# Pooled attention with a hierarchical mixture of experts: the router's weights, the guess of the first expert, one copy chain, one subtraction and one down piece change places in a hand-written order

## The chip, the cores and the metric

The kernel runs on one core of one Trainium2 chip. The metric is the device time of one execution in microseconds (us). Engines are named as in the profile: PE (matmuls; PEld is its weight load), DVE, ACT, POOL, and SP, which issues most of the transfers.

## The reference

Eight batches of attention whose k and v are averaged over groups of 8 positions (576 positions become 72), and behind them a mixture of 4 groups of 4 experts that sends each of the 4608 tokens to one expert.

```python
k_p = k.reshape(B, H, Sp, pool, D).mean(axis=3)          # 8, 8, 72, 64
v_p = v.reshape(B, H, Sp, pool, D).mean(axis=3)
scores = scale * np.matmul(q, k_p.transpose(0, 1, 3, 2))
scores = scores - np.max(scores, axis=-1, keepdims=True)
attn = np.exp(scores)
attn = attn / (np.sum(attn, axis=-1, keepdims=True) + 1e-09)
x = np.matmul(attn, v_p)                                 # then (4608, 512)
...
g_idx = np.argmax(x @ w_group, axis=1)                   # group of each token
...
e_idx = np.argmax(xg @ w_expert[g], axis=1)              # expert within the group
...
h = np.maximum(xg[mask_e] @ w1[g, e], 0.0)               # 512 -> 1024
out[tok_idx] = combined[:, None] * (h @ w2[g, e])        # 1024 -> 512
```

## The kernel before

**Tiling.** A batch has 576 tokens in five chunks (four of 128, one of 64), two chunks side by side in the scores' tiles. One expert, guessed from the mean of v, is computed for all tokens of a batch; the tokens that chose another expert are done at the end. Each fp32 operand of the up (512 to 1024) and down (1024 to 512) matmuls is cut into a high and a low part, and a product is made of three matmuls.

**The order is written by hand.** Four strings name small pieces of work, and `run` calls them one by one; the scheduler keeps that order on each engine, so a piece's instructions stand on each engine's list where the string has it. START opens batch 0's attention and fetches the first expert's weights; FIRST is the rest of batch 0 with its experts, together with batch 1's attention; STEADY serves batches 1 to 6 and LAST batch 7. In them `a` and `m` are the attention and the experts of the batch at hand, `n` and `w` those of the next one, `x` the attention after that, `t` the router's weights and the idle matmuls.

**The pieces that matter here**, with the profile's lines:

- `load_wr` fetches the router's weights by two transfers that ACT issues (L894 the groups', 8 KB, L895 the experts', 32 KB; tile `ht`). `turn_wr` transposes them on PE (L901), `put_wr` copies them (L904, ACT).
- `qt`, `qta`: q of one chunk transposed (L298, PE) and copied (L304, ACT). `sc`: scores (L320, PE). `mx`, `sb`: maximum and its subtraction (L326, L333, DVE). `ex`: exponential (L337, ACT). `su_`: sums and reciprocals (L342 to L344, DVE). `nm`: division (L349, POOL). `pt`: transpose (L355, DVE).
- `vr`: sums of v over 8 positions (L223 is the last addition on POOL). `rep`: these sums repeated over the partitions by matmuls (L244, L247, PE); `repa` and `repd` copy them (L253, ACT; L261, DVE).
- `guess_x` (L483 on PE, a copy L485 on ACT) and `guess_e` (L491 on PE; then DVE from L494 to L472 and L475): the expert of most tokens, guessed. SP reads its number, and `load` (L549) fetches its weights in pieces of 512 KB.
- `av`: probabilities by v (L375, PE), here in two runs for each batch: `av:0:1` and `av:2:4` in batch 0, `av:0:4` in two parts in batch 1. `ava` takes the high part (L389, ACT), `avd` the low one (L393, DVE).
- `split`: high part of an expert's weights (L556, ACT); `spd`: their low part (L562 on DVE, L566 on POOL). `up` (L579, PE), `ua` (L584, ACT), `upd` (L589, DVE).
- `down:z`: 8 matmuls (L618; L623 for the last chunk); z counts in threes through the chunks, so 0 to 2 are chunk 0, 9 to 11 chunk 3; 12 and 13 are the last chunk. `da` takes a finished chunk from PSUM (for the last chunk ACT L634, DVE L635, ACT L636).
- `warm:z`: z matmuls whose result nobody reads (L911).

Tiles of one name go round in a pool (`mm` and `sc` in PSUM): a piece that opens one waits until the one before it in that place has been read.

Of the kernel before, what the change touches and what calls it, by code (L numbers as in the profile page):

```python
# [34 lines left out]
TCARGS = dict(schedule_with_timeline_sim=True)  # L35

START = """
a.load_k:1:w a.load_k:0:w a.load_q:0 a.qt:0 a.load_r:k a.load_r:v a.load_q:1 a.kr:0:r a.kr:1:p a.load_v:0 a.load_v:1 a.rr:r a.qta:0 a.load_q:3 a.kt
n.load_r:v t.load_wr a.kta a.qt:1 a.load_q:4 a.vr:0:r a.sc:0 a.mx:0 t.turn_wr a.qta:1 a.vr:1:p a.sc:1 a.load_q:2 t.warm:2 a.sb:0 n.load_r:k a.ex:0
n.load_k:0 a.mx:1 t.put_wr a.sb:1 a.su_:0 a.qt:3 a.ex:1 a.rep a.guess_x a.nm:0:p a.su_:1 a.repd:1 a.repa:1 a.nm:1:p n.load_v:1 a.pt:0 a.repa:0 a.qt:2  # L40
a.repd:0 a.qta:3 n.load_k:1 a.pt:1 a.guess_e n.kr:0:r a.av:0:1 a.ava:0:0 a.ava:0:1 a.avd:0:1 a.ava:0:3 a.qt:4 m.load:1:1 m.load:1:2 m.load:1:3
a.ava:0:2 a.qta:2 a.sc:3 a.avd:0:3 a.avd:0:0 m.load:1:0 a.avd:0:2 n.kr:1:p a.mx:3 a.sb:3 m.split:1:1 a.ex:3 n.load_qb:3 m.spd:1:1:v n.load_qb:1 a.sc:2
a.su_:3 t.warm:4 a.nm:3:p a.qta:4 t.warm:7
"""
FIRST = """
m.split:1:3 a.mx:2 m.up:2:0 n.load_qb:2 m.split:1:2 m.ua:2:0 a.sc:4 a.sb:2 t.warm:8 m.spd:1:2:p m.up:3:0 a.pt:3 m.up:4:0 m.up:5:0 a.ex:2 a.mx:4 a.sb:4
# [5 lines left out]
m.split:2:2 x.load_k:0 x.load_qb:0 m.up:3:1 x.load_k:1 m.ua:6:1 m.ua:3:1 n.ex:1 x.load_v:1 m.split:2:0 n.su_:0 a.count m.up:1:1 n.repa:1 m.up:2:1  # L52
m.upd:6:1 n.sc:3 n.repd:1 m.split:2:1 n.sc:4 m.ua:2:1 n.su_:1 m.up:0:1 a.keep_x m.ua:1:1 n.repd:0 n.nm:0:p m.upd:3:1 n.nm:1:p m.upd:2:1 m.spd:2:1:p
m.up:5:1 m.up:4:1 n.mx:4 n.pt:0 m.upd:1:1 n.mx:3 m.spd:2:0:p n.pt:1 m.down:0 n.sb:3 n.sb:4 m.ua:5:1 n.ex:3 m.ua:0:1 n.ex:4 m.ua:4:1 m.upd:5:1
m.upd:0:1 n.su_:4 m.spd:2:2:p n.nm:4:p m.upd:4:1 a.gex n.su_:3 n.nm:3:p m.down:12 x.kr:1:p n.pt:4 m.down:13 n.pt:3 n.av:0:4:0 n.av:0:4:1 x.load_qb:2
x.load_qb:1 n.ava:0:1 x.kr:0:r x.load_v:0 m.down:1 x.rr:r a.gates n.ava:0:4 n.ava:0:0 n.ava:0:3 n.ava:0:2 n.avd:0:4 n.avd:0:0 x.vr:1:p n.avd:0:3
m.da:4 n.avd:0:2 m.down:2 n.xr:0 m.down:9 n.xr:3 x.kt x.qb:0 n.ava:0:5 n.avd:0:1 n.avd:0:5 x.kta n.xr:2 m.down:6 x.vr:0:r x.sc:0 n.xr:1 n.rt x.rep
x.mx:0 x.sb:0 n.route x.repa:0 x.repd:1 m.down:10 n.main_expert w.load:1:0 x.ex:0 m.da:0 n.gex w.load:1:1 x.su_:0 m.down:11 x.repa:1 w.load:1:3
m.down:3 m.down:4 w.load:1:2 x.qb:1 x.repd:0 m.down:7 n.gates w.load:2:1 w.split:1:0 m.da:3 w.load:2:0 x.nm:0:p m.down:5 w.spd:1:0:v n.keep_x x.pt:0
# [902 lines left out]
```

## Time and profile before

| what | value |
|---|---|
| three executions | 550.5, 552.46, 553.12 us; median 552.46 |
| the profiled execution | 555.95 us, of which span from first to last instruction 554.3 |
| mean granted clock of PE | 0.994 of full speed |
| PE busy | 532.4 us, 96% of the span |
| DVE, POOL, ACT busy | 359.2 (65%), 275.7 (50%), 214.9 us (39%) |
| chain that ended last | PE 89%, DVE 5%, DMA 2%, ACT 1%, issue 1% |

The chain that ended last is followed back from the last instruction to what released it, step by step, and its shares say which engine the time was spent on. PE is idle for some 22 us, and its slices of busy time in the profile's second part are under 9 tenths only at the opening and at the end.

### The profile page before, as it was taken

What the parts mean: (1) busy time and instruction counts of PE and PEld (TensorE: products, weight loads), DVE (VectorE), ACT (ScalarE), POOL (GpSimd) and SP (SyncE); (2) the same over time, 40 slices, a digit from 0 to 9 for tenths busy, and PEclk for the clock granted to TensorE, in tenths of its full rate; (3) what the DMA queues carried; (4) which work ended last, traced back from release to release, by engine and by line L of the source; (5) the groups of instructions that cost most, each with busy time, mean ns of one, the idle gap of its engine ahead of it and who ended that gap; (6) DMA issues with size and microseconds to landing.
All of it is one profiled execution on the core that took longest, in us unless ns stands there. A gap on an engine that the chain in (4) does not pass through costs nothing.

```text
span 554.3 us, 15239 instructions
## 1 busy us (share of the span) xinstructions
PE 532.4 (96%) x6218; PEld 472.7 (85%) x6218; DVE 359.2 (65%) x940; ACT 214.9 (39%) x402; POOL 275.7 (50%) x259
## 2 busy tenths in 40 slices
PE   4889998999999999999999999999999999999995
PEld 3789987799888998899888998899888997899874
DVE  4688897678385946858485946857485944347520
ACT  2254523245324543345334533354324532344111
POOL 3527386116942668046933678146933654165400
PEclk9999998999999999999999999999999999999998
DMA  9778561299108751389109740499309000634801
GB/s 235 157 187 199 144 124 51 92 304 203 40 21 290 209 97 56 124 275 192 41 20 332 181 103 35 151 392 201 58 20 355 19 1 21 235 136 182 293 22 72
DMA packets 115649, 81.32 MB, mean 147 GB/s; under 512 B 73562, under 2 KB 92250, under 8 KB 115192
## 3 DMA queue, kind: packets, MB, share of 16 engines
q1 hardware_dynamic: 110256, 70.92, 46.0%
q10 hardware_dynamic: 5288, 9.35, 4.5%
q8 instruction: 50, 0.82, 0.6%
q14 instruction: 23, 0.19, 0.1%
q0 software_dynamic: 32, 0.04, 0.0%
HBM read 75.01 MB, written 28.38 MB: 187 GB/s over the span
## 4 chain that ended last, share of the span: by engine, by line
PE 89%; DVE 5%; DMA 2%; ACT 1%; issue 1%; POOL 0%; SPq 0%; POOLq 0%
PE mm L579 35%; PE mm L618 31%; PE sc L375 5%; PE mm L623 5%; PE sc L320 4%; PE tp L409 1%; DMA rem<-in_k_dram 1%; DMA ht<-in_moe_w_expert_dram 1%; PE mm L598 1%; PE sc L244 1%; PE mm L911 1%; DVE su L342 1%; DVE p L333 1%; DVE mx L326 1%; DVE pT L355 1%
## 5 line engine op out<-in xcount | busy, mean ns | idle before, releaser
L579 PE MATMUL mm<-xt,w 128*128 128x256 f32 (+1 forms) x1536 | 214.9, 298 | 0.1
L579 PEld LDWEIGHTS mm<-xt,w 128*128 128x128 f32 x1536 | 206.5, 189 | 5.4 <-DVE ht L589 1.8
L618 PE MATMUL mm<-w,ht 128*128 128x512 f32 x744 | 177.9, 394 | 0.0
L566 POOL TENSOR_TENSOR w<-sw,w 128x512 fp32r<-128x512 f32 x94 | 120.5, 1307 | 92.9 <-ACT w L556 62.7
L618 PEld LDWEIGHTS mm<-w,ht 128*128 128x128 f32 x744 | 137.5, 188 | 31.1 <-issue 2.8
L349 POOL TENSOR_TENSOR p<-p,su 128x576 f32<-128x576 f32 (+1 forms) x40 | 45.8, 1152 | 124.6 <-DVE su L344 117.4
L589 DVE SCALAR_TENSOR_TENSOR ht<-mm,ht 128x256 fp32r<-128x256 f32 x192 | 57.5, 342 | 65.6 <-ACT ht L584 65.4
L584 ACT ACTIVATE ht<-mm 128x320 fp32r<-128x320 f32 (+1 forms) x128 | 51.3, 412 | 109.8 <-PE mm L579 109.3
L556 ACT CAST w<-sw 128x1024 fp32r<-128x1024 f32 x64 | 66.1, 1045 | 20.0 <-DMA sw<-in_moe_w_dram 19.9
L326 DVE TENSOR_REDUCE mx<-sc 128x8 f32<-128x576 f32 (+1 forms) x40 | 29.8, 745 | 34.3 <-PE sc L320 34.3
L400 POOL TENSOR_TENSOR sw<-xt 128x640 f32<-128x640 f32 (+1 forms) x28 | 39.1, 1426 | 10.5 <-DVE xt L393 10.4
L218 POOL TENSOR_TENSOR kv<-kv 128x512 f32<-128x512 f32 x21 | 32.0, 1524 | 9.6 <-DMA kv<-in_v_dram 7.5
L337 ACT ACTIVATE p<-p 128x576 f32<-128x576 f32 (+1 forms) x40 | 27.3, 682 | 23.1 <-DVE p L333 21.7
L375 PE MATMUL sc<-pT,v 32*64 32x128 f32 (+11 forms) x1560 | 33.3, 297 | 2.7 <-issue 2.0
L355 DVE STREAM_TRANSPOSE pT<-p 128x576 f32<-128x576 f32 (+1 forms) x40 | 30.6, 764 | 7.3 <-POOL p L349 7.2
L631 ACT ACTIVATE y<-mm,gm 128x512 f32<-128x512 f32 x31 | 21.3, 689 | 31.8 <-PE mm L618 23.1
L375 PEld LDWEIGHTS sc<-pT,v 32*64 32x64 f32 (+3 forms) x1560 | 28.5, 143 | 6.0 <-issue 3.8
L623 PE MATMUL mm<-w,ht 128*128 128x512 f32 x128 | 31.7, 391 | 0.0
L342 DVE TENSOR_REDUCE su<-p 128x8 f32<-128x576 f32 (+1 forms) x40 | 29.4, 735 | 3.2 <-ACT p L337 3.2
L333 DVE TENSOR_TENSOR p<-sc,mx 128x576 f32<-128x576 f32 (+1 forms) x40 | 29.9, 748 | 1.0
L320 PE MATMUL sc<-kT,qT 64*64 64x72 f32 x1264 | 28.3, 237 | 1.5 <-DVE xt L393 1.4
L389 ACT CAST xt<-sc 128x480 fp32r<-128x480 f32 (+3 forms) x36 | 18.0, 542 | 29.7 <-PE sc L375 15.5
(217 smaller groups left out, 490.9 us busy)
## 6 DMA issues: line engine op xcount, KB each, us to landing
sw<-in_moe_w_dram SPq DMA_DIRECT2D x72, 512.0 KB
xscr<-xt SPq DMA_DIRECT2D x8, 2304.0 KB
kv<-in_v_dram SPq DMA_DIRECT2D x16, 512.0 KB
q<-in_q_dram SPq DMA_DIRECT2D x112, 72.0 KB
out_dram<-y ACTq DMA_DIRECT2D x31, 256.0 KB
kv<-in_k_dram SPq DMA_DIRECT2D x14, 512.0 KB
kv<-in_moe_w_dram SPq DMA_DIRECT2D x6, 512.0 KB
pT<-xscr SPq DMA_DIRECT2D x2, 1152.0 KB
```

The lines of the kernel that those rows point to most:

```text
L320: nc.tensor.matmul(ps[t:t + 64, y, SP * g:SP * g + SP], lhsT=s.qT[c][r, g, w:w + 64], rhs=k, start=True, stop=True)
L349: (nc.vector if eng == "v" else nc.gpsimd).tensor_tensor(out=pf, in0=pf, in1=bc(sf, SP), op=ALU.mult)
L355: nc.vector.transpose(out=s.pT[0:n, :, 32 * c:32 * c + 32], in_=s.p[c].rearrange("p u x s -> p (u x s)").rearrange("p (b i) -> p b i", i=3 ...
L375: nc.tensor.matmul(to[64 * x:64 * x + 64], lhsT=w, rhs=s.pT[e, k, 32 * c0:32 * c0 + n], start=(z == 0), stop=(z == 2))
L400: nc.gpsimd.tensor_tensor(out=x, in0=a, in1=b, op=ALU.add)
L556: nc.scalar.copy(out=wh, in_=raw)
L566: nc.gpsimd.tensor_tensor(out=wl[:, p], in0=raw[:, p], in1=wh[:, p].bitcast(F32), op=ALU.subtract)
L579: nc.tensor.matmul(ps[:, 0:n], lhsT=l[:, kc, fs], rhs=xt[:, r, kc, sl], start=(kc == 0 and i == 0), stop=(kc == 3 and i == 2))
L584: nc.scalar.activation(out=s.ht[f][:, o:o + n], in_=s.pu[f, hf][:, 0:n], func=AF.Relu)
L589: stt(out=ht[:, at:at + hi - lo], in0=ps[:, lo - o:hi - o], scalar=0.0, in1=ht[:, lo:hi].bitcast(F32), op0=ALU.max, op1=ALU.subtract)
L618: nc.tensor.matmul(ps, lhsT=s.ht[f][:, 640 * l + o:640 * l + o + 128], rhs=s.w[2, f // 2][r][:, f % 2, :], start=(i == 0), stop=(i == 23))
L623: nc.tensor.matmul(ps, lhsT=s.ht[f][:, 512:640], rhs=s.w[2, f // 2][r][:, f % 2, :], start=(i == 0), stop=(i == 15))
```

## The change

START is rewritten and two lines of FIRST are; no piece is added, and only `t.warm:7` becomes `t.warm:3`. In the diff, moved pieces have shifted the line breaks:

```diff
 START = """
-a.load_k:1:w a.load_k:0:w a.load_q:0 a.qt:0 a.load_r:k a.load_r:v a.load_q:1 a.kr:0:r a.kr:1:p a.load_v:0 a.load_v:1 a.rr:r a.qta:0 a.load_q:3 a.kt
-n.load_r:v t.load_wr a.kta a.qt:1 a.load_q:4 a.vr:0:r a.sc:0 a.mx:0 t.turn_wr a.qta:1 a.vr:1:p a.sc:1 a.load_q:2 t.warm:2 a.sb:0 n.load_r:k a.ex:0
-n.load_k:0 a.mx:1 t.put_wr a.sb:1 a.su_:0 a.qt:3 a.ex:1 a.rep a.guess_x a.nm:0:p a.su_:1 a.repd:1 a.repa:1 a.nm:1:p n.load_v:1 a.pt:0 a.repa:0 a.qt:2
-a.repd:0 a.qta:3 n.load_k:1 a.pt:1 a.guess_e n.kr:0:r a.av:0:1 a.ava:0:0 a.ava:0:1 a.avd:0:1 a.ava:0:3 a.qt:4 m.load:1:1 m.load:1:2 m.load:1:3
-a.ava:0:2 a.qta:2 a.sc:3 a.avd:0:3 a.avd:0:0 m.load:1:0 a.avd:0:2 n.kr:1:p a.mx:3 a.sb:3 m.split:1:1 a.ex:3 n.load_qb:3 m.spd:1:1:v n.load_qb:1 a.sc:2
-a.su_:3 t.warm:4 a.nm:3:p a.qta:4 t.warm:7
+t.load_wr a.load_k:1:w a.load_k:0:w a.load_q:0 a.qt:0 a.load_r:k a.load_r:v a.load_q:1 a.kr:0:r a.kr:1:p a.load_v:0 a.load_v:1 a.rr:r a.qta:0
+a.load_q:3 a.kt n.load_r:v a.kta a.qt:1 a.load_q:4 a.vr:0:r a.sc:0 a.mx:0 t.turn_wr a.qta:1 a.vr:1:p a.sc:1 a.load_q:2 t.warm:2 a.sb:0 n.load_r:k
+a.ex:0 n.load_k:0 a.mx:1 t.put_wr a.sb:1 a.su_:0 a.ex:1 a.guess_x a.qt:3 a.rep a.nm:0:p a.su_:1 a.repd:1 a.repa:1 a.nm:1:p n.load_v:1 a.pt:0 a.repa:0
+n.load_k:1 a.guess_e a.qt:2 a.repd:0 a.qta:3 a.pt:1 n.kr:0:r a.av:0:1 a.ava:0:0 a.ava:0:1 a.avd:0:0 a.ava:0:2 a.qt:4 m.load:1:1 m.load:1:2 m.load:1:3
+a.ava:0:3 a.qta:2 a.sc:3 a.avd:0:1 a.avd:0:2 m.load:1:0 a.avd:0:3 n.kr:1:p a.mx:3 m.split:1:1 m.spd:1:1:v a.sb:3 a.ex:3 n.load_qb:3 n.load_qb:1 a.sc:2
+a.su_:3 t.warm:4 a.nm:3:p a.qta:4 t.warm:3
 """
 FIRST = """
...
-m.upd:0:1 n.su_:4 m.spd:2:2:p n.nm:4:p m.upd:4:1 a.gex n.su_:3 n.nm:3:p m.down:12 x.kr:1:p n.pt:4 m.down:13 n.pt:3 n.av:0:4:0 n.av:0:4:1 x.load_qb:2
-x.load_qb:1 n.ava:0:1 x.kr:0:r x.load_v:0 m.down:1 x.rr:r a.gates n.ava:0:4 n.ava:0:0 n.ava:0:3 n.ava:0:2 n.avd:0:4 n.avd:0:0 x.vr:1:p n.avd:0:3
+m.upd:0:1 n.su_:4 m.spd:2:2:p n.nm:4:p m.upd:4:1 a.gex n.su_:3 n.nm:3:p m.down:12 x.kr:1:p n.pt:4 m.down:13 m.down:1 n.pt:3 n.av:0:4:0 n.av:0:4:1
+x.load_qb:2 x.load_qb:1 n.ava:0:1 x.kr:0:r x.load_v:0 x.rr:r a.gates n.ava:0:4 n.ava:0:0 n.ava:0:3 n.ava:0:2 n.avd:0:4 n.avd:0:0 x.vr:1:p n.avd:0:3
```

The edits by number: (1) `load_wr` goes to the very front; (2) `guess_x` goes ahead of `qt:3` and `rep`, and `guess_e` ahead of `qt:2`, `repd:0` and `pt:1`; (3) the copies behind `av:0:1` go 0, 1, 2, 3 on ACT and on DVE, where they went 0, 1, 3, 2 on ACT and 1, 3, 0, 2 on DVE, so that two of DVE's stand ahead of nothing that `sc:3` waits for; (4) `split:1:1` and `spd:1:1:v` go ahead of `sb:3`; (5) four matmuls of `warm` fall away; (6) `down:1` goes ahead of batch 1's `av:0:4`.

On PE, in the opening, the order before (`ident` is the identity by which q is transposed, `vp` and `rp` the sums of v, `tp` the guess's tile, `wr` the router's weights):

```order
L911 MATMUL mm<-ones 128x128 x2
L298 MATMUL mm<-ident,q 128x128 x4
L244 MATMUL sc<-vp,four 128x256 x4
L247 MATMUL sc<-rp,four 128x64 x2
L483 MATMUL tp<-selg,vp 64x4 x4
L483 MATMUL tp<-selg,rp 64x4
L483 MATMUL tp<-selg,vp 64x4 x4
L483 MATMUL tp<-selg,rp 64x4
L298 MATMUL mm<-ident,q 128x128 x4
L491 MATMUL tp<-wr,ht 128x20 x4
L375 MATMUL sc<-pT,v_312 64x64
```

and of the changed kernel at the same place:

```order
L911 MATMUL mm<-ones 128x128 x2
L483 MATMUL tp<-selg,vp 64x4 x4
L483 MATMUL tp<-selg,rp 64x4
L483 MATMUL tp<-selg,vp 64x4 x4
L483 MATMUL tp<-selg,rp 64x4
L298 MATMUL mm<-ident,q 128x128 x4
L244 MATMUL sc<-vp,four 128x256 x4
L247 MATMUL sc<-rp,four 128x64 x2
L491 MATMUL tp<-wr,ht 128x20 x4
L298 MATMUL mm<-ident,q 128x128 x4
L375 MATMUL sc<-pT,v_312 64x64
```

The first half of the guess (L483) has passed one q transpose and v's repeated sums, the second half (L491) one more q transpose; the first `av` (L375) keeps its place.

On DVE, in the opening, one piece of the difference (`v_310` is v's repeated sums, `pT` the transposed probabilities of chunk 1, `xt` the attention's output, `w` a weight's low part, `moh` the guess):

```order
 L472 TENSOR_SCALAR me<-ct 128x1
 L475 TENSOR_SCALAR moh<-cr,ct 128x16
+L261 TENSOR_TENSOR v_310<-sc,mask 128x128
+L355 STREAM_TRANSPOSE pT<-p 128x18x32
 L215 TENSOR_REDUCE kp<-kv 128x128
 L393 TENSOR_TENSOR xt<-sc,xt 128x4x2x32 x4
 L326 TENSOR_REDUCE mx<-sc 128x8
+L562 TENSOR_TENSOR w<-sw,w 128x1024
 L333 TENSOR_TENSOR p<-sc,mx 128x2x4x72
-L562 TENSOR_TENSOR w<-sw,w 128x1024
 L342 TENSOR_REDUCE su<-p 128x8
 L343 TENSOR_SCALAR su<-su 128x8
```

The two instructions that batch 0's first `av` waits for now stand behind the whole guess, and the weights' subtraction stands between the maximum and the subtraction of chunk 3.

On PE, at batch 1's `av`, the order before (`v_1062` and `v_1180` are batch 1's v):

```order
L320 MATMUL sc<-kT,qT 64x72 x32
L579 MATMUL mm<-xt,w 128x320 x36
L618 MATMUL mm<-w,ht 128x512 x8
L623 MATMUL mm<-w,ht 128x512 x16
L375 MATMUL sc<-pT,v_1062 64x160
L375 MATMUL sc<-pT,v_1180 64x160
```

and now:

```order
L320 MATMUL sc<-kT,qT 64x72 x32
L579 MATMUL mm<-xt,w 128x320 x36
L618 MATMUL mm<-w,ht 128x512 x8
L623 MATMUL mm<-w,ht 128x512 x16
L618 MATMUL mm<-w,ht 128x512 x8
L375 MATMUL sc<-pT,v_1058 64x160
```

Eight of the 24 down matmuls that stood behind the `av` now stand ahead of it. The orders on POOL and SP are as before.

## Rows read from the trace of the kernel before

**Rows 1.** Waits of PE, whole run: us in all, times, longest.

```profile
PE sc L375 <- issue: 2.0, 1, 2.0
PE mm L901 <- DMA ht<-in_moe_w_expert_dram: 1.8, 1, 1.8
```

**Rows 2.** Chain that ended last, opening: start us, us, what.

```profile
9.64 6.03 DMA ht<-in_moe_w_expert_dram
...
18.76 0.85 PE mm L298 x4
19.62 1.17 PE sc L244 x8
...
21.09 2.51 PE tp L483 x20
...
26.45 0.58 PE sc L375 x18
```

**Rows 3.** Timeline from 14 to 32 us: start, us, instruction, [idle before <-releaser].

```profile
16.96 0.46 POOL L223 TENSOR_TENSOR vp<-kv 128x128 f32<-128x128 f32 x1
...
24.42 1.74 PE L491 MATMUL tp<-wr,ht 128*128 128x20 f32 x8
...
25.32 0.29 DVE L261 TENSOR_TENSOR v<-sc,mask 128x128 f32<-128x128 f32 x1 [2.46 <-ACT v L253]
...
26.23 0.15 DVE L494 TENSOR_REDUCE m<-tp 128x5 f32<-128x20 f32 x1
...
27.74 0.23 DVE L475 TENSOR_SCALAR moh<-cr,ct 128x16 f32<-128x16 f32 x1
...
28.86 2.39 SPq L549 DMA_DIRECT2D sw<-in_moe_w_dram  x4
```

**Rows 4.** Timeline from 28 to 46 us.

```profile
29.56 1.20 ACT L389 CAST xt<-sc 128x256 fp32r<-128x256 f32 x4 [3.78 <-PE sc L375]
...
30.24 1.64 DVE L393 TENSOR_TENSOR xt<-sc,xt 128x256 fp32r<-128x256 f32 x4 [0.45 <-ACT xt L389]
...
31.70 2.50 PE L320 MATMUL sc<-kT,qT 64*64 64x72 f32 x64 [1.42 <-DVE xt L393]
...
33.28 0.76 DVE L326 TENSOR_REDUCE mx<-sc 128x8 f32<-128x576 f32 x1 [1.40 <-PE sc L320]
34.08 0.76 DVE L333 TENSOR_TENSOR p<-sc,mx 128x576 f32<-128x576 f32 x1
...
34.75 1.22 DVE L562 TENSOR_TENSOR w<-sw,w 128x1024 fp32r<-128x1024 f32 x1
34.93 0.68 ACT L337 ACTIVATE p<-p 128x576 f32<-128x576 f32 x1 [1.45 <-DVE p L333]
...
35.88 0.75 DVE L342 TENSOR_REDUCE su<-p 128x8 f32<-128x576 f32 x1
...
39.51 0.75 DVE L326 TENSOR_REDUCE mx<-sc 64x8 f32<-64x576 f32 x1 [0.33 <-PE sc L320]
...
45.84 0.29 PEld L375 LDWEIGHTS sc<-pT,v 32*64 32x64 f32 x23 [0.30 <-DVE pT L355]
```

**Rows 5.** Timeline of PE and DVE around batch 1's av.

```profile
82.81 1.86 PE L375 MATMUL sc<-pT,v 32*64 32x160 f32 x90 [0.39 <-DVE pT L355]
86.64 2.07 PE L375 MATMUL sc<-pT,v 32*64 32x128 f32 x56 [1.97 <-issue]
...
90.01 5.75 PE L618 MATMUL mm<-w,ht 128*128 128x512 f32 x24
...
92.50 0.68 DVE L635 TENSOR_TENSOR y<-mm,y 64x512 f32<-64x512 f32 x1
```

**Rows 6.** One window: us; busy (instructions) of PE, PEld, DVE, ACT, POOL; PEclk, DMA share, GB/s.

```profile
86.60:90.00 3.40, 3.36 (x102) 2.97 (x101) 1.05 (x5) 0.56 (x1) 0.40 (x1) 0.52 0.20 77
```

**Rows 7.** DMA queues, window 28 to 29 us: packets, MB, share of 16 engines.

```profile
q8 instruction: 1, 0.02, 5.9%
```

**Rows 8.** DMA queues, window 29 to 37 us; no other queue moved anything.

```profile
q1 hardware_dynamic: 2187, 2.04, 83.0%
```

**Rows 9.** DMA queues, window 84 to 85 us; no other queue moved anything.

```profile
q8 instruction: 1, 0.02, 6.0%
```

## Prediction

> **What bounds the kernel now.** Read the busy shares first: PE works 532.4 of 554.3 us, and the chain that ended last is 89% PE, so a change pays only where PE stands idle or where it makes PE do less. The second view is therefore PE's waits over the whole run. Two of them lie where the diff works: 1.8 us for the router's weights and 2.0 us in batch 1's `av`, in which the profile names no releaser, only "issue" [rows 1]. The third view is the opening's chain, in order of time: it shows that the router's second transfer is issued at 9.64 and lands 6.03 later, and what PE does from there to the first `av` at 26.45 [rows 2]. Last the timelines of the three places that the diff touches [rows 3 to 5]. There the reader should look at which engine's idle time ends on which: at 31.70 PE waits for DVE's L393, at 33.28 DVE waits for PE's scores, and at 45.84 PE's second `av` waits for DVE's pT [rows 4]. From 33 to 46 us the opening is bound by DVE's softmax, not by PE.
>
> **Edit 1, the router's weights first.** Issued at the front instead of at 9.64, the 6.03 us of the transfer [rows 2] lie under the loads of k and v. PE's wait of 1.8 us [rows 1] goes, and all that follows on PE can start 1.81 earlier (1.8 as printed): `qt:3` would stand at 16.95 instead of 18.76 [rows 2]. The price: 40 KB go ahead of k's load. At the mean rate that rows 8 give, 2.04 MB in 8 us or 0.255 MB per us, that is 0.16 us. The bounds are nothing and 0.2; I take 0.1. The Trainium skill says in DMA: Bandwidth & Descriptors, section Issuing engines are not separate DMA queues, that a transfer that ACT issues runs on the same 16 engines as SP's and mixes with them, so a separate issuer would not spare k this delay; no run here shows it yet.
>
> **Edit 2, the guess.** `guess_x` takes 2.51 [rows 2] and now stands ahead of `qt:3` (0.85) and `rep` (from 19.62 to 21.09, 1.47) [rows 2]. From 16.95 it ends at 19.46, `qt:3` at 20.3, `rep` at 21.8, and `guess_e` (1.74, [rows 3]) at about 23.5, where it ended at 26.16: 2.6 earlier. POOL's last sum of v is ready at 17.42 [rows 3]; if the guess's first matmul has to wait for it, 0.5 of that goes. I take 2.5. From L494 at 26.23 to the weights' issue at 28.86 it is 2.63 [rows 3], so the expert's weights are asked for at about 26.3.
>
> But `av:0:1` gets nothing of this. It starts 1.13 us after L261 (25.32 to 26.45, [rows 2, 3]), and L261 now stands behind the guess's chain on DVE. That chain runs from 26.23 to 27.97, 1.74 us [rows 3]; started at 23.7 it ends at 25.4, so L261 starts within 0.1 of its old time, and `av` too. What is gained is spent as idle time of PE ahead of `av`: 1.81 from the wait, plus whatever the order of the two q transposes moves.
>
> **Edits 3 to 5, the copies, the subtraction, the warm matmuls.** DVE's four L393 take 1.64, 0.41 each; ACT's four L389 take 1.20, 0.30 each [rows 4]. `sc:3` now waits for two of the former instead of three, and the first of them for one copy instead of two: 0.41 + 0.30 = 0.71, so L320 goes from 31.70 to 31.0 and `mx:3` from 33.28 to 32.6 [rows 4]. Behind it the subtraction L562, 1.22 [rows 4], now comes ahead of `sb:3`. Before, ACT's exponential (L337, 0.68, from 34.93) lay under L562 and the sums followed at once, at 35.88 [rows 4]. Now nothing covers the exponential. From `mx:3` to L337 it was 1.65 (33.28 to 34.93), L562 holds DVE for 1.13 (34.75 to 35.88), and the exponential takes 0.68 [rows 4]: 32.6 + 1.65 + 1.13 + 0.68 = 36.06. So 0.71 forward becomes 0.18 late: edit 4 puts 0.9 back on DVE's chain. What returns is the 0.33 for which `mx:4` waited for PE [rows 4]: with scores 0.7 earlier and eight of 22 idle matmul records gone PE is ready sooner. Sum for DVE's chain to the second `av`: 0.18 - 0.33 + 0.1 for edit 1 = -0.05 for the whole of START. Bounds: +0.3 if `mx:4`'s wait stays, -2.5 if everything that edit 2 gains is passed on. I stay at the small end, since the engine that PE waits for at 45.84 is DVE [rows 4], whose work there is unchanged.
>
> **Edit 6, the down piece.** The 24 matmuls behind `av` take 5.75 [rows 5], so the eight of `down:1` take 1.92. Ahead of `av` they cover PE's 0.39 wait for pT [rows 5]; `av` starts and ends 1.92 - 0.39 = 1.53 later. Behind it 1.92 us of cover are gone. `down:9` opens a new `mm` tile, and for that DVE's L635 must have read the last chunk; L635 stands behind copies of `av`'s results and ends at 93.18, 3.17 after `av` (90.01) [rows 5]. Before, 3.83 us of `down:1` and `down:2` lay there; now 1.92 do, so PE waits 3.17 - 1.92 = 1.25. In all -0.39 + 1.25 = +0.87 us, and `av`'s copies, the router and the next loads are late by as much. The bounds are -0.39 (another place of the pool is free) and +0.87; the rows say that L635 ended only 0.66 ahead of its need, so I take +0.87. Nothing in PE's waits behind it is long enough to take it back [rows 1].
>
> **The 2 us that nobody explains.** After 90 records of this `av` PE stops for 1.97 us, and at once the 102 records from 86.60 to 90.00 run at a granted clock of 0.52, that is 1.2 of 2.4 GHz [rows 5, 6]. At 84 to 85 us the only thing that moves is one packet of PE's own instructions [rows 9]. So PE ran out of instructions. In count of instructions nothing changes: eight records of `warm` and their eight weight loads fall away ahead, eight matmuls of `down:1` with eight loads come, and `av` stands as far down PE's list as before. If the place decides, the stall comes again. The Trainium skill says, in Runtime: NRT & Kernel Launch, section Instruction fetch mechanics, that instructions stream in blocks of 16 KiB, 256 of them, and that the crossing of a block is mostly hidden. This one is not: one packet of 0.02 MB and 1.97 us of stall stand in rows 5 and 9. By the rule alone the stall would be an accident of one execution, and the sum would lack it.
>
> **The sum.** START -0.05, edit 6 +0.87: +0.82 us on the profiled execution, from 555.95 to about 556.8. That execution lies 3.5 us above the median of the three runs, 552.46; by the same difference the forecast is 552.46 + 0.82 = 553.3 us. Three runs of one kernel spread from 550.5 to 553.12, so I call 0.5%, 2.8 us, what a measurement can tell from no change.
>
> **The rivals.**
>
> *A, the sum as it stands* (0.47): 553.3, with a range of its own from 551.5 to 554.9.
>
> *B, the stall goes* (0.22): with `down:1` ahead, `av` starts 1.5 us later by the clock while PE is fed by longer matmuls; if the packet comes at a time rather than at a place, it comes under `down:1`. Then 1.97 go, and the slow stretch too: 102 records at the 1.86 / 90 of the records before the stall [rows 5] are 2.1 us instead of 3.36 [rows 6], 1.26 less. Together -3.2 + 0.82 = -2.4: 550.1. For it speaks that the stall is single in the run [rows 1]; against it that the count of instructions is unchanged.
>
> *C, slower: instructions come late in the opening* (0.20). The packet at 28 to 29 us [rows 7] passed just ahead of the weights, issued at 28.86 [rows 3]. From 29 to 37 us, while they take 83% of the transfer engines, no instruction packet comes [rows 8]. With the weights asked for at 26.3 that packet falls into their traffic. From packet to going on the other stall took over 1.6 us (at latest 85 to 86.64, [rows 5, 9]), so a packet landing after about 29.4 makes `sc:3` at 31.0 late. If it waits until the traffic ends, some 7 us after the issue, PE goes on at about 36, 5 us late; if it merely shares, nothing is lost. Its middle is some 3 us: 556.3. The decision is whether such a packet queues behind 2 MB or goes between.
>
> *D, the opening passes everything on* (0.11): DVE's chain from 33 to 46 is not the bound, because it waited for weights somewhere that the rows put down to another engine. Then -2.5 + 0.1 + 0.87 = -1.5 gives 550.9.
>
> **How the numbers follow.** The likeliest is A, 553.3. The range from 549.2 to 556.4 holds A, D, most of B and the nearer part of C; outside are B with D together (547) and the far end of C (558). Faster than 549.7: 0.11 of B (half of it, alone or with D), 0.04 of D, 0.04 of A where stall and pool both fall well, 0.19, and 0.04 where B gives back more than rows say: 0.23 in all. Slower than 555.2: 0.15 of C, 0.07 of A where edits 4 and 6 cost more: 0.22. The rest, 0.55, is within the bound.
>
> **What the changed profile would show.** Right: no wait of L901 for DMA; L549 issued near 26.3; a wait of 1.5 to 2 us of L375 for DVE at an `av` that still starts at about 26.4; the sums L342 of chunk 3 near 36; the second `av` near 45.6; no wait for pT at batch 1's `av`, the same "issue" of about 2 us after 90 records with the clock near 0.5 behind it, and a wait of about 1.2 us at the first L618 of `down:9`. Wrong: that issue gone or put elsewhere (B), a new "issue" between 27 and 37 us (C), the second `av` at 43 to 44 (D), or `down:9` without a wait.

## The result and the profile after

The changed kernel takes 554.87 us (median of 12 executions, 553.74 to 556.96), the kernel before 552.17 (12 executions, 549.68 to 554.31): a ratio of 1.0056, with a 95% interval from 1.0037 to 1.0075. It is slower by 2 to 4 us, where the forecast had 0.82; the time lies in the forecast range.

The two profiled executions don't show that: 555.95 before, 556.84 after. The first was one of the longest of the kernel before, as two more traces of it show below, so the place of the loss cannot be read from this pair alone.

PE's waits of the changed kernel (us in all, times, longest); they answer to [rows 1]:

```profile
PE sc L320 <- issue: 2.6, 1, 2.6
PE sc L375 <- DVE pT L355: 2.4, 1, 2.4
PE mm L618 <- DVE y L635: 1.2, 1, 1.2
PE sc L320 <- DVE xt L393: 0.9, 1, 0.9
```

L901's wait for the router's weights is gone, and so is the issue in batch 1's `av`. Three new waits stand in their place. The first two lie in the opening. Its timeline, the answer to [rows 3] and [rows 4]:

```profile
24.11 0.18 DVE L494 TENSOR_REDUCE m<-tp 128x5 f32<-128x20 f32 x1 [0.99 <-PE tp L491]
...
25.13 1.26 POOL L218 TENSOR_TENSOR kv<-kv 128x512 f32<-128x512 f32 x1 [3.48 <-DMA kv<-in_k_dram]
...
25.23 1.20 DVE L475 TENSOR_SCALAR moh<-cr,ct 128x16 f32<-128x16 f32 x1
26.34 0.28 DVE L261 TENSOR_TENSOR v<-sc,mask 128x128 f32<-128x128 f32 x1
26.35 2.11 SPq L549 DMA_DIRECT2D sw<-in_moe_w_dram  x4
...
27.45 3.21 PE L375 MATMUL sc<-pT,v 32*64 32x64 f32 x192 [2.45 <-DVE pT L355]
...
32.14 0.50 PE L320 MATMUL sc<-kT,qT 64*64 64x72 f32 x4 [0.86 <-DVE xt L393]
...
35.27 2.19 PE L320 MATMUL sc<-kT,qT 64*64 64x72 f32 x60 [2.63 <-issue]
36.54 0.76 DVE L326 TENSOR_REDUCE mx<-sc 128x8 f32<-128x576 f32 x1 [3.89 <-PE sc L320]
...
39.91 0.75 DVE L342 TENSOR_REDUCE su<-p 128x8 f32<-128x576 f32 x1 [0.81 <-ACT p L337]
```

Read it from the guess. The expert's weights are asked for at 26.35, 2.5 us earlier than before, as worked out. The price stands beside it: L261 and pT come after the guess's chain, whose last instruction L475 takes 1.20 us where it took 0.23 [rows 3], so PE waits 2.45 us and starts `av` at 27.45. Then `sc:3` stops after four of its 64 records for 2.63 us of issue. The second `av` starts at 49.43, against 45.84 [rows 4].

The DMA queues of the changed kernel, first from 26 to 32.9 us (no other queue moved anything), then the tenth of a microsecond behind it:

```profile
q1 hardware_dynamic: 1769, 1.76, 78.4%
```

```profile
q1 hardware_dynamic: 30, 0.03, 85.6%
q8 instruction: 1, 0.02, 64.5%
```

The packet of PE's instructions comes at 32.9, behind 1.76 MB, and PE goes on 2.3 us later. That q8 is PE's queue is inferred: it moves 0.82 MB in 50 packets in an execution, the only other instruction queue 0.19 MB, and PE has some 12,400 of the 15,200 instructions. Before it came at 28 to 29, ahead of the weights [rows 7]. This is rival C.

Around batch 1's `av` (timeline of PE; answers to [rows 5]):

```profile
85.91 1.98 PE L618 MATMUL mm<-w,ht 128*128 128x512 f32 x8
87.81 2.81 PE L375 MATMUL sc<-pT,v 32*64 32x160 f32 x146
...
91.24 2.11 PE L618 MATMUL mm<-w,ht 128*128 128x512 f32 x8
94.55 2.08 PE L618 MATMUL mm<-w,ht 128*128 128x512 f32 x8 [1.20 <-DVE y L635]
```

`down:1` covers the wait for pT, `down:2` follows, and the first matmul of `down:9` waits 1.20 us for L635: edit 6 as forecast, but for the stall, which is not there.

### The profile page after: what moved, and what is told of

It reads as the page before. It is cut to its first block, busy times and chain, and to the rows that moved or that the text cites. A ratio compares the mean times of both kernels' runs of the same rounds, so it can differ in the third digit from the quotient of the medians.

```text
span 555.2 us, 15222 instructions
## 1 busy us (share of the span) xinstructions
PE 531.6 (96%) x6210; PEld 471.1 (85%) x6210; DVE 360.3 (65%) x940; ACT 214.6 (39%) x402; POOL 275.6 (50%) x259
## 4 chain that ended last, share of the span: by engine, by line
PE 87%; DVE 6%; DMA 3%; issue 1%; ACT 1%; SPq 0%; POOL 0%; ACTq 0%; POOLq 0%; DVEq 0%
PE mm L579 35%; PE mm L618 29%; PE mm L623 5%; PE sc L375 5%; PE sc L320 4%; PE tp L409 1%; DMA rem<-in_v_dram 1%; PE mm L598 1%; DMA out_dram<-y 1%; PE sc L244 1%; DVE p L333 1%; DMA sw<-in_moe_w_dram 1%; DVE mx L326 1%; DVE pT L355 1%; DVE su L342 1%
## 5 line engine op out<-in xcount | busy, mean ns | idle before, releaser
L326 DVE TENSOR_REDUCE mx<-sc 128x8 f32<-128x576 f32 (+1 forms) x40 | 29.7, 743 | 32.9 <-PE sc L320 32.9
L218 POOL TENSOR_TENSOR kv<-kv 128x512 f32<-128x512 f32 x21 | 32.0, 1525 | 10.6 <-DMA kv<-in_v_dram 7.1
L375 PE MATMUL sc<-pT,v 32*64 32x128 f32 (+11 forms) x1560 | 31.7, 290 | 2.6 <-DVE pT L355 2.4
L375 PEld LDWEIGHTS sc<-pT,v 32*64 32x64 f32 (+3 forms) x1560 | 27.2, 139 | 5.8 <-issue 4.3
L342 DVE TENSOR_REDUCE su<-p 128x8 f32<-128x576 f32 (+1 forms) x40 | 29.5, 737 | 4.0 <-ACT p L337 4.0
L320 PEld LDWEIGHTS sc<-kT,qT 64*64 64x64 f32 x1264 | 24.2, 142 | 8.3 <-issue 3.5
```

Source lines behind the costliest of these rows:

```text
L320: nc.tensor.matmul(ps[t:t + 64, y, SP * g:SP * g + SP], lhsT=s.qT[c][r, g, w:w + 64], rhs=k, start=True, stop=True)
L375: nc.tensor.matmul(to[64 * x:64 * x + 64], lhsT=w, rhs=s.pT[e, k, 32 * c0:32 * c0 + n], start=(z == 0), stop=(z == 2))
```

## The experiments

**The edits of START alone.** FIRST is that of before; against the changed kernel:

```diff
-m.down:13 m.down:1 n.pt:3 n.av:0:4:0
+m.down:13 n.pt:3 n.av:0:4:0
...
-x.load_v:0 x.rr:r a.gates
+x.load_v:0 m.down:1 x.rr:r a.gates
```

> Edits 1 to 5 alone, the down piece where it was. Theory O (the opening is what costs): the first av starts about 1.0 us later than before (27.45, since L475 lasts 1.2 us under POOL's L218), and sc:3 stops for about 2.6 us of issue in executions where PE's instruction packet falls behind the expert's weights. The second av is then at 46.8 without the stop and 49.4 with it; with the stop in about half of the executions the time is some 1.9 us over the kernel before, near 554.1. Rival D6 (the down piece is what costs): no difference, 552.2.

Measured: 554.49 us, ratio 1.0055 (1.0037 to 1.0072). The opening alone carries the whole loss: with edit 6 on top of it the ratio is 1.0056. In its profiled execution the stop in `sc:3` is shorter, 0.87 us, and the second `av` comes at 46.60:

```profile
25.12 0.22 DVE L475 TENSOR_SCALAR moh<-cr,ct 128x16 f32<-128x16 f32 x1
...
25.39 1.27 POOL L218 TENSOR_TENSOR kv<-kv 128x512 f32<-128x512 f32 x1 [3.85 <-DMA kv<-in_k_dram]
...
26.37 3.23 PE L375 MATMUL sc<-pT,v 32*64 32x64 f32 x192 [1.48 <-DVE pT L355]
...
32.45 2.19 PE L320 MATMUL sc<-kT,qT 64*64 64x72 f32 x60 [0.87 <-issue]
```

Here POOL's L218 begins only after L475 has ended, L475 takes 0.22, and `av` starts 1.1 us ahead of the 27.45 that theory O had.

**Edit 6 alone**, with the opening of before; against the kernel before:

```diff
-m.down:13 n.pt:3 n.av:0:4:0
+m.down:13 m.down:1 n.pt:3 n.av:0:4:0
...
-x.load_v:0 m.down:1 x.rr:r a.gates
+x.load_v:0 x.rr:r a.gates
```

> Edit 6 alone, the opening as before. Theory O: PE waits 1.2 us at the first L618 of down:9 and no longer for pT, so the time is 0.5 to 0.9 us over the kernel before, near 552.9; whether the issue of 2 us in batch 1's av comes is open. Rival D6: nearly the whole 2.7 us, near 554.9.

Measured: 552.57 us, ratio 1.0016 (0.9996 to 1.0035), that is +0.9 us with an interval from -0.2 to +1.9. That is the size that theory O had, though zero is not excluded. The wait at `down:9` is 1.2 us, and there is no issue.

**The guess behind pT again, on DVE alone.** `guess_e` is cut in two; its matmuls stay where the change put them.

```diff
-a.guess_e a.qt:2 a.repd:0 a.qta:3 a.pt:1 n.kr:0:r
+a.guess_e a.qt:2 a.repd:0 a.qta:3 a.pt:1 a.guess_d n.kr:0:r
```

> The changed kernel, with the guess's DVE instructions behind L261 and pT of chunk 1 again (PE's order as in the changed kernel). Theory O: the first av starts at about 25.0 instead of 27.45, the weights are asked for at 27 to 27.5 instead of 26.35, PE's instruction packet comes ahead of their traffic (near 27.5), no issue of over 1 us in sc:3, and the second av near 45 instead of 49.4; time near 551, some 3.5 us under the changed kernel and 1 us under the kernel before. Rival D6: the opening is covered, 554.9 as the changed kernel.

Measured: 552.00 us, ratio 1.0005 (0.9988 to 1.0021): 2.9 us under the changed kernel by the medians, with every other edit in place. The forecast 551 was 1 us too low. Its opening:

```profile
23.31 0.29 DVE L261 TENSOR_TENSOR v<-sc,mask 128x128 f32<-128x128 f32 x1 [0.56 <-ACT v L253]
...
24.57 3.23 PE L375 MATMUL sc<-pT,v 32*64 32x64 f32 x192
...
26.43 2.82 SPq L549 DMA_DIRECT2D sw<-in_moe_w_dram  x4
...
29.27 1.39 PE L320 MATMUL sc<-kT,qT 64*64 64x72 f32 x64 [1.07 <-DVE xt L393]
...
34.27 2.65 PE L579 MATMUL mm<-xt,w 128*128 128x256 f32 x12 [1.85 <-ACT qT L304]
...
38.13 0.75 DVE L326 TENSOR_REDUCE mx<-sc 64x8 f32<-64x576 f32 x1 [0.84 <-PE sc L320]
```

The weights are asked for at 26.43, as early as in the changed kernel, and nothing stops in `sc:3`. PE has its instruction packet at 26.5, as the DMA queues from 26.5 to 26.6 us show:

```profile
q8 instruction: 1, 0.02, 59.1%
```

So early weights are no harm by themselves. Against the changed kernel `av` starts 2.9 us earlier and the stop of 2.6 is gone; of these 5.5 us, 5.0 are left at the second `av`, 44.46, since PE now waits 1.85 us for q and `mx:4` 0.84 us for PE.

**POOL's sums of batch 1's k behind chunk 3's division.**

```diff
-m.load:1:0 a.avd:0:3 n.kr:1:p a.mx:3
+m.load:1:0 a.avd:0:3 a.mx:3
...
-a.nm:3:p a.qta:4
+a.nm:3:p n.kr:1:p a.qta:4
```

> The changed kernel, with POOL's three additions for batch 1's k (L218, L219, L223) behind chunk 3's division instead of under the guess. Theory P (L475 lasts as long as POOL's L218 runs beside it): L475 takes about 0.2 us instead of 1.20, L261 starts near 25.4 and the first av near 26.5 instead of 27.45; the weights are asked for at 26.3 as in the changed kernel, so the late packet stays, and the time is near 554. Rival: L475's 1.2 us has another cause and stays, av at 27.4, and the time is 554.9 or more, since k's sums come later.

Measured: 556.51 us (6 executions), ratio 1.0088 (1.0056 to 1.0121). Theory P's place is right and its time is wrong. L475 takes 0.23 and `av` starts at 26.52; the packet stays late, with a stop of 1.78:

```profile
25.27 0.23 DVE L475 TENSOR_SCALAR moh<-cr,ct 128x16 f32<-128x16 f32 x1
...
26.52 3.21 PE L375 MATMUL sc<-pT,v 32*64 32x64 f32 x192 [1.48 <-DVE pT L355]
...
33.34 2.18 PE L320 MATMUL sc<-kT,qT 64*64 64x72 f32 x60 [1.78 <-issue]
...
46.68 0.78 DVE L355 STREAM_TRANSPOSE pT<-p 128x576 f32<-128x576 f32 x1 [0.60 <-POOL p L349]
```

The sums moved into the softmax's part of POOL, and pT then waits for POOL's division. Less their stops the second `av`s start at 46.81 here and at 46.80 in the changed kernel, so what the first `av` gained is given back. The median is 1.6 us higher than that of the changed kernel, but the two intervals overlap.

**Three of four weight pieces held back.**

```diff
-m.load:1:1 m.load:1:2 m.load:1:3
+m.load:1:1
...
-m.load:1:0 a.avd:0:3
+a.avd:0:3
...
-n.load_qb:3 n.load_qb:1 a.sc:2
+n.load_qb:3 m.load:1:2 m.load:1:3 m.load:1:0 n.load_qb:1 a.sc:2
```

> The changed kernel, with three of the first four pieces of the expert's weights asked for behind four loads of q (at 31 us and later) instead of at once at 26.35; all other engines' orders as in the changed kernel. Theory W (PE's instruction packet is late because it stands behind 2 MB of weights): with one piece of 512 KB in the way the packet comes by about 30, there is no issue of over 0.5 us in sc:3, and the second av starts near 46.5; time 1 us or more under the changed kernel, near 553.5. Rival N (the packet's lateness has nothing to do with that traffic): the issue of 0.9 to 2.6 us in sc:3 stays, and the time is 554.9 or, since the weights come later, more.

Measured: 555.22 us, ratio 1.0049 (1.0024 to 1.0075). The packet comes at 29.5 and `sc:3` runs through, as theory W said. The time is as rival N said, for another reason: the weights are now what is waited for.

```profile
31.11 2.78 PE L320 MATMUL sc<-kT,qT 64*64 64x72 f32 x64 [0.86 <-DVE xt L393]
...
38.98 1.99 ACT L556 CAST w<-sw 128x1024 fp32r<-128x1024 f32 x2 [2.40 <-DMA sw<-in_moe_w_dram]
...
45.74 2.71 PE L579 MATMUL mm<-xt,w 128*128 128x256 f32 x12 [1.24 <-DVE ht L589]
```

`mx:3` comes at 32.98 instead of 36.54, but ACT's split waits 2.40 us for the weights, and the second `av` starts at 48.37.

**Edit 4 undone** in the changed kernel.

```diff
-m.split:1:1 m.spd:1:1:v a.sb:3 a.ex:3 n.load_qb:3
+a.sb:3 m.split:1:1 a.ex:3 n.load_qb:3 m.spd:1:1:v
```

> The changed kernel with edit 4 undone: chunk 3's subtraction ahead of the weights' again. If the exponential that nothing covers costs what the prediction has (0.9 us on DVE's chain), the time from mx:3 to the sums L342 goes from 3.4 to about 2.6 us, the second av comes 0.8 to 0.9 us earlier, and the time is near 554.1. Rival: the weights' subtraction is what is waited for next, and the time stays at 554.9 or rises.

Measured: 553.69 us, ratio 1.0038 (1.0018 to 1.0059), 1.2 us under the changed kernel by the medians, though the two intervals overlap. From `mx:3` at 34.57 to the sums at 37.17 it is 2.60, against 3.37 with edit 4. The forecast step of 0.9 us measures 0.8.

**Edits 1, 2 on PE, 3 and 5 alone**: the guess behind pT on DVE as above, and edits 4 and 6 undone as above. Then the same with `qt:3` ahead of `guess_x`:

```diff
-a.guess_x a.qt:3 a.rep
+a.qt:3 a.guess_x a.rep
```

> The order with edits 1, 2 (on PE), 3 and 5 alone: guess on DVE behind pT of chunk 1, chunk 3's subtraction first, the down piece where it was. Theory: first av at 24.6 as with the guess behind pT, the sums L342 of chunk 3 at 32.9 instead of 34.0, no wait of mx:4 for PE, the second av near 42.5 where it is 44.5 with edits 4 and 6; no wait at the first L618 of down:9. Time near 549.5, faster than the kernel before by 0.4%. Rival: PE or the weights bind the opening by then, second av at 44, time 551.5.

> As the one with edits 1, 2 (on PE), 3 and 5 alone, with qt:3 ahead of guess_x again, where PE waits about 2 us for POOL's last sum of v: the first av up to 0.8 us earlier, near 23.8, and the time up to 0.8 us lower, near 549. Rival: L261 and pT wait for ACT's copies and not for PE, and nothing moves.

Measured: 552.86 us, ratio 1.0016 (0.9993 to 1.0039), and 550.72 us, ratio 0.9976 (0.9954 to 0.9999). Both lie above what was forecast, 549.5 and 549. The second is the one order whose interval lies under 1, and barely; as the best of several orders it may owe that to chance. The second `av` starts at 43.73 and 43.20. Their openings are 0.7 and 1.3 us ahead of the one with edits 4 and 6, and not all of it reaches the end: in both profiled executions PE runs out of instructions in batch 1's `av`, for 1.8 and 1.5 us. Behind the stop the rest of this `av` took 3.09 us in the first (84.94 to 88.03) and 1.78 in the second (84.14 to 85.92): the granted clock was 0.56 there in the one and 1.00 in the other. PE's waits of the second:

```profile
PE sc L375 <- issue: 1.5, 1, 1.5
...
PE sc L375 <- DVE pT L355: 0.8, 1, 0.8
```

**The kernel before, two more traces.**

> The kernel before once more, unchanged, for a second trace. Theory V (the profiled execution of before was one of its long ones: its opening ran late and PE ran out of instructions in batch 1's av): the first av starts near 25.2 as in the run of edit 6 alone, not 26.45, the second near 44.5, not 45.84, and the time is 551 to 553. Rival: the same marks as in the first trace, 26.4 and 45.8.

> The same again, a third trace. If edit 6 takes away an issue that the kernel before really has, the issue of 1.4 to 2.0 us in batch 1's av stands in both of these traces, as in the three others with the down piece behind the av; if it was an accident of one execution, it stands in at most one.

Measured: 550.68 and 552.36 us, one execution each. Neither has an issue in batch 1's `av`. Their openings, one execution each:

```profile
21.15 0.73 PE L483 MATMUL tp<-selg,vp 128*64 128x4 f32 x8
...
24.59 0.29 DVE L261 TENSOR_TENSOR v<-sc,mask 128x128 f32<-128x128 f32 x1 [1.60 <-ACT v L253]
...
25.71 3.21 PE L375 MATMUL sc<-pT,v 32*64 32x64 f32 x192 [1.12 <-DVE m L494]
```

```profile
20.70 0.63 PE L483 MATMUL tp<-selg,vp 128*64 128x4 f32 x8
...
24.04 0.29 DVE L261 TENSOR_TENSOR v<-sc,mask 128x128 f32<-128x128 f32 x1 [1.02 <-ACT v L253]
...
25.16 3.23 PE L375 MATMUL sc<-pT,v 32*64 32x64 f32 x192 [0.80 <-DVE m L494]
```

The first `av`s start 0.7 and 1.3 us ahead of the one that the prediction counted with, and the second `av`s at 45.27 and 44.80 instead of 45.84. The stall stood in one of the three traces. The same L483 in the first trace:

```profile
21.02 1.02 PE L483 MATMUL tp<-selg,vp 128*64 128x4 f32 x8
```

**Edit 6 without its wait:** the last chunk's `da:4` ahead of the copies.

```diff
-x.load_qb:2 x.load_qb:1 n.ava:0:1 x.kr:0:r x.load_v:0 x.rr:r a.gates n.ava:0:4
+x.load_qb:2 x.load_qb:1 x.kr:0:r x.load_v:0 a.gates m.da:4 n.ava:0:1 n.ava:0:4
...
-m.da:4 n.avd:0:2
+x.rr:r n.avd:0:2
```

> Edits 1, 2 (on PE, qt:3 ahead of guess_x), 3, 5 and 6, and the last chunk's da:4 ahead of the av's copies (gates ahead of it, the sum rr of k and v behind the third copy), so that down:9 finds its tile free. Theory: the first av near 24.8, the second near 43.2, no issue over 0.5 us and no wait for pT at batch 1's av, no wait at the first L618 of down:9; time 1 to 2 us under the same opening without edit 6 (550.72), near 549.2. Rival: kt's transposes wait for rr or the copies are late, and the gain is given back: 550.7.

Measured: 554.10 us, ratio 1.0048 (1.0029 to 1.0067): the rival's way, and 3.4 us past its time. The 16 matmuls behind `av` run through, and then PE waits for what was pushed back:

```profile
84.78 3.92 PE L618 MATMUL mm<-w,ht 128*128 128x512 f32 x16
88.55 0.38 PE L268 MATMUL tp<-ident,kp 128*128 128x128 f32 x2
90.99 0.33 PE L264 MATMUL tp<-ident,rp 64*64 64x64 f32 x4 [2.06 <-DVE rp L215]
93.08 3.65 PE L618 MATMUL mm<-w,ht 128*128 128x512 f32 x8 [1.75 <-DVE xt L393]
```

A wait of 1.2 us is saved and waits of 3.8 are paid. The last eight matmuls took 3.65 us instead of some 2.1, since the granted clock was 0.53 there (window 93.08 to 96.73) after the two waits.

**Edit 5 undone** in the fastest order: `t.warm:7` again.

> The fastest order so far (edits 1, 2 on PE with qt:3 first, 3 and 5), with edit 5 undone: warm:7 again. Theory: the eight records fill time in which PE waits for DVE, so mx:4 waits for PE by at most 0.3 us as in the kernel before, the second av comes between 43.2 and 43.6, and the time is within 0.5 us of 550.7. The place at which PE runs out of instructions in batch 1's av, if it does, goes back from 98 records to 90, since eight records and their eight weight loads more stand ahead of it. Rival: PE binds the opening by then, the second av is 1.2 us later (44.4), 551.9.

Measured: 551.58 us, ratio 0.9995 (0.9975 to 1.0014), 0.9 us over 550.7 where at most 0.5 was forecast. The second `av` starts at 43.94, 0.3 past the upper bound of theory, `mx:4` waits 0.53 for PE, and no issue stands in batch 1's `av`. The interval overlaps that of the order with `warm:3`: whether edit 5 is worth anything is not settled.

## Why the prediction was right or wrong

The sign and the range held, but not by the forecast's mechanism; the step of START failed. The sum's sign came from edit 6, whose cost no run tells from zero, and the loss came from START, which the sum had at nothing; the range held because it was wide enough for part of rival C. The prediction's own signs of being wrong stand in the changed profile: a new issue between 27 and 37 us (C), and the old one gone (B). That the two profiled executions differ by 0.89 us, near the forecast 0.82, is luck: START's loss, 3.6 us at the second `av`, met a trace of before that had lost 2 us in batch 1's `av`.

**START, -0.05 forecast.** The run of these edits alone gives 554.49 against 551.68, +2.8 us. Two of the prediction's sentences made the error.

- "`av` gets nothing of this", because L261 "starts within 0.1 of its old time". The new time was worked out well: L261 was forecast at 25.4 and starts at 25.25 to 25.41 in four runs with the change's order, `av` at 26.4 to 26.5 (27.45 in the changed kernel, where L475 is stretched). The old time was read from one execution, 25.32. In the further traces of before L261 starts at 24.59 and 24.04 and `av` about a microsecond ahead of those four runs. The sum was made against an execution that had already lost what the edit costs. What it had lost goes with PE's clock: the eight L483 took 0.63 to 0.73 us in three of the four traces with the START of before, that of edit 6 alone among them, where the granted clock from 22 to 24 us was 0.89 to 1.00, and 1.02 in the first. In all ten traces with a rewritten START eight L483 that run through took 1.0 us; in the one with the guess behind pT the clock from 18 to 24 us shows as 0.50. Whether the rewritten order keeps the clock low there was not tested. At the same low clock the guess's chain in front of L261 costs 1.5 to 2.1 us: behind pT it leaves L261 at 23.31 and 23.79.
- Rival C was given 0.20 and taken out of the sum. It came about in each run in which `av` comes late and the weights early: stops of 2.63, 0.87, 1.78 and 1.56 us in the four runs with that order and all four pieces asked for at once, none in the ten other profiled executions. The price of 3 us was near the worst of them. The condition was stated wrongly: not "a packet lands after 29.4 because weights are asked for at 26.3", since the order with the guess behind pT asks at 26.43 and has its packet at 26.5. The traces fit another one: whether PE gets to the place in its list where the packet is fetched before the weights' traffic begins. In eight of the nine traces where the weights are asked for after `av` has started, the packet comes 1.8 to 2.0 us behind `av`'s start (2.3 in the first trace of before); in the five where they are asked for ahead of it, by 0.1 to 1.1 us, it comes 3.1 to 5.5 us behind. An `av` that starts late then costs twice: PE stands idle ahead of it, and the packet comes late.

Putting the guess behind pT on DVE takes both away and brings the time from 554.87 to 552.00. That shows the step, the guess's chain ahead of L261 and pT. The share of each, about 1 us for the late `av` and between 0.9 and 2.6 for the stop, is read from the traces, of which there is one for each run. That the weights' traffic is what holds the packet is supported by the times above, not shown: with one piece in the way the packet came at 29.5, with four at 29.8, 30.8, 31.0 and 32.9. The first two are close.

**Edits 1 and 3** went the way that was forecast: no wait of L901, and PE's wait for L393 at `sc:3` fell from 1.42 to 0.86, by 0.56 where 0.71 was forecast. Edit 1's price was too low, 0.1 with 0.2 as the bound: the first maximum of the scores (L326) starts 14.55 to 14.80 us into the span in the ten traces with the router's weights first and at 14.29 to 14.42 in the four without, some 0.3 us later. **Edit 4**, 0.9 us on DVE's chain, measured 0.8. **Edit 5** cost nothing that these runs can measure.

**Edit 6, +0.87.** PE's wait at `down:9` was forecast as 1.25 and is 1.2 in every run with the edit as it stands; alone it gives +0.9 (-0.2 to +1.9), which agrees with the forecast and does not exclude zero. On top of START's edits it adds nothing that these runs can measure (1.0055 without it, 1.0056 with it). The wait is shown; its price in time is not.

**The stall of 2 us.** The forecast kept it in both kernels (A) and gave B 0.22 for its going. It is absent from the changed kernel, as B said, but also from two of three traces of before, so little of it was in the median to be gained. Its place is a matter of count: behind 90 records in the two executions with as many instructions ahead as before, behind 98 or 99 in the three with eight `warm` records less and the down piece behind `av`. Whether PE stops there depends on when the packet came: with `av` from 82 to 84 it came at 84.2 in the execution of [rows 5, 9], at 79.9 and 76.4 in the other two of before. Why it came late in that one, with no other transfer under way [rows 9], stays open.

The rule on instruction fetch that the prediction weighed, Runtime: NRT & Kernel Launch, section Instruction fetch mechanics of the Trainium skill, says that the crossing of a block is mostly hidden. Most are: the profile's page counts 50 packets of q8 in an execution. But in eight of the fourteen profiled executions PE stopped on issue for 0.9 to 2.6 us behind such a packet, in the run of START's edits alone twice, and the forecast left the opening's stop out of its sum.

## What to carry to other kernels

When one engine's chain is moved ahead of another's, the price is what stands behind it on that engine, counted against several traces and not against the one at hand: an execution that was late there already hides the cost. A transfer that starts earlier can push back traffic that nobody wrote into the program, so look at what else must come through in that window, instruction packets included. Here being late at such a packet cost twice, the wait and the stop. And before two traces are compared, compare what the same matmuls took in each: one had its opening at the low clock, by its durations, and that looked like an effect of the order.

## What the runs showed of the hardware

**Instructions.** From the packet to the going on of PE it was 2.3 to 2.9 us in each of the nine stops: in `sc:3` 32.9 to 35.27 in the changed kernel and 29.8 to 32.45, 31.0 to 33.34 and 30.8 to 33.30 in runs with its opening; in batch 1's `av` 84.2 to 86.64 before, and 84.8 to 87.47, 82.7 to 85.62, 82.2 to 84.94 and 81.5 to 84.14 in four runs.

**DVE beside POOL.** L475 took 1.20 us where POOL's L218 had begun 0.10 us earlier, and ended within 0.05 us of it (26.43 and 26.39); with L218 moved away it took 0.23. In the first trace of before L499 took 0.60 and ended with POOL's L219 (27.43 and 27.40). Elsewhere L475 took 0.89, 1.23, 1.09 and 1.31 us and L499 1.25 under an L218 and ended 0.02 to 0.04 us behind it (third trace of before; edits 1, 2, 3 and 5 in both orders and with `warm:7`; edit 6 alone). Not every DVE instruction under a POOL one is stretched: L472 took 0.15 in the changed kernel, where it started 0.03 us behind L218. The Trainium skill, SBUF — State Buffer, section SBUF: two separate sides, says that DVE in a two-port mode or with two SBUF inputs and POOL share a pair of ports as an exclusive lock, held for a whole instruction; the nearly equal ends of L475 and L218 agree with that, and no run here tells the port from another cause.

**PE's speed in the opening.** The same 64 matmuls of `sc:3` took 2.50 us in the profiled execution of before, 2.32 in its second trace and 1.39 with the guess behind pT. Windows over them (us, busy and instructions of PE, PEld, DVE, ACT, POOL, granted clock, DMA share, GB/s), one trace each in that order:

```profile
31.70:34.20 2.50, 2.50 (x65) 2.33 (x65) 1.06 (x3) 1.05 (x1) 0.00 (x0) 1.00 0.83 235
```

```profile
30.96:33.28 2.32, 2.32 (x65) 2.18 (x65) 1.07 (x3) 1.00 (x1) 0.00 (x0) 0.50 1.05 356
```

```profile
29.27:30.66 1.39, 1.39 (x65) 1.31 (x65) 1.02 (x3) 0.56 (x2) 0.00 (x0) 1.00 0.95 274
```

The second ran at 1.2 GHz and the third at 2.4 by the column. The first is as slow as the second although the column says 1.00, as it does for the whole opening of that execution, so in an opening the durations have to be read beside the clock.
